# Token factors and first weights made beside the experts, one batch's gating at the attention's end, re-paired PSUM banks

## The chip, the cores and the metric

One core of a Trainium2 chip. The metric is the device time of one execution in microseconds, lower is better. The engines are TensorE (PE, with its weight loads as PEld), VectorE (DVE), ScalarE (ACT), GpSimd (POOL) and SyncE (SP), which here only issues transfers.

## The reference

Linear attention, a mixture of experts with one expert per token, and a feed-forward block, in float32, on 4 batches of 576 tokens with 8 heads of 64:

```python
def phi(x):                       # omega: 128 x 64
    h = x @ omega.T - (x * x).sum(-1, keepdims=True) / 2
    return np.exp(h - h.max(-1, keepdims=True)) / np.sqrt(128)
q_p, k_p = phi(q_s), phi(k_s)
kv, z = k_p^T @ v, k_p.sum(2)     # per batch and head
x = (q_p @ kv) / (q_p @ z + 1e-6) # then 2304 tokens x 512
e = argmax(x @ w_gate)            # 8 experts, softmax weight g
x = g * (relu(x @ w1[e]) @ w2[e]) # 512 -> 1024 -> 512
out = relu(x @ w_in) ** 2 @ w_out # 512 -> 2048 -> 512
```

## The kernel before

Products that need float32 accuracy are made of three fp32r products: each operand is split into a rounded part, which ScalarE copies, and a remainder, which VectorE subtracts (`split`, L688). A split so costs one instruction on each of the two engines, and PE waits for both.

**Attention** (`attention`, L430 on) runs over 18 tiles of 128 tokens; a step `s` works on several tiles at different depths. Since 576 is no multiple of 128, tiles 4 and 13 hold tokens of two batches; `kv_part` (L277) multiplies 64 rows of them for the one batch and 64 for the other. When a batch's logits are complete, `gating` (L387) makes its one-hot choice of experts on DVE, `counting` (L417) sums it with small matmuls and `counted` (L427) gives the batch's commonest expert to POOL as a register. For batches zero and one this is done inside the loop (gating at s = 7 and 11, counting at s = 8 and 12), for two and three beside the first expert steps.

**Experts**: the kernel computes, for each batch, its commonest expert for all of its tokens (another path computes the general case when a token differs, and isn't taken here). The work is 64 steps (batch, half of its tokens, f of 8). `ffn_next` issues layer one of the coming step and its `hidden` part (L765 on ACT, hh; L766 on DVE, hl); `ffn_this` issues layer two of the present step, 24 matmuls in all per step, and then `extras`: what the table that `plan` (L812) made has for this step. Before the first step of another half, `xsplit` (L740, L742) splits four pieces of x. `layer2` (L767) copies y at the last f of a half from PSUM with ACT and stores it to memory (yscr).

**Feed-forward**: blocks of its first product are made with a seven-product scheme: sums of quarter blocks (`lefts`, `rights`, L60 to L72, on POOL), then seven products. 16 stages `first(u)` (L916) of some 11 us have 14 pieces of six matmuls; stages 0 and 1 use the token factors of batches zero and one, stages 2 and 3 those of two and three. A token factor of half (b, c) is loaded from yscr (`x_load`), summed (`x_sums`, POOL) and split (`x_split`); a weight pair likewise (`pair_load`, `pair_sums`, `pair_split`). `raw_place` gives the unsplit data one of two places in turn. The table puts the loads of batches zero and one at steps 48 to 54 and of two and three beside stages 0 and 1. The other DVE work of the expert steps is narrowing of weights (`narrow`, L716 to L720) and the remainder of the expert weights (`wB`, L612).

The second product (`plain`, `second`, L1044) is written in groups of two tiles; the last groups use seven products again, which lie two to a PSUM bank (`PRODS`). `close` (L1065) adds them on DVE, scales by ACT (L1090) and stores by SP (L1091).

The order of each engine's instructions is the order in which this code issues them; the table's step numbers (SA + n is a piece of the feed-forward stages, 14 per stage) fix it.

Of the kernel before, what the change touches and what calls it, by code (L numbers as in the profile page):

```python
# [7 lines left out]
F32 = mybir.dt.float32  # L8
# [7 lines left out]
P = 128  # L16
# [10 lines left out]
KC = DM // P  # L27
VW = D + 1
# [12 lines left out]
PRODS = ((1, 0, 0, 0, 0), (6, 4, 4, 1, 0), (7, 5, 5, 1, 1), (5, 3, 3, 2, 0), (3, 6, 1, 2, 1), (4, 1, 6, 3, 0), (2, 2, 2, 0, 1))  # L41
# [48 lines left out]
class Kern:  # L90
# [36 lines left out]
    def setup_attn(self):  # L127
# [9 lines left out]
        self.hl, self.three = {}, {}  # L137
        w = self.qpool.tile([P, 2 * M], F32, name="wom")
# [29 lines left out]
    def load_v(self, t):  # L168
        if t >= NT:
            return  # L170
        v = self.vin[t] = self.kpool.tile([P, H, VW], F32, tag="vin", name=f"vin{t}", bufs=5)
        self.nc.sync.dma_start(out=v, in_=self.a["vv"][t])
# [104 lines left out]
    def kv_part(self, b, t, i):  # L277

        nc = self.nc
# [3 lines left out]
        lo, hi = [(lo, hi) for bb, lo, hi in pieces(t) if bb == b][0]  # L283
        for j in range(4):
            nc.tensor.matmul(  # L285
                self.kv_ps[b, i][:, j * VW : (j + 1) * VW],
                self.kp[t][lo:hi, 4 * i + j, :],
                self.vin[t][lo:hi, 4 * i + j, :],
# [127 lines left out]
    def counting(self, b):  # L416

        nc = self.nc
        ps = self.banks(f"cnt_ps{b}")[:, 0, :] if b > 1 else self.bank("x", f"cnt_ps{b}")
# [20 lines left out]
    def attention(self, beside):  # L440
# [13 lines left out]

        def gating(last):
            self.gating((0, 5, 9, 14)[(4, 8, 13, 17).index(last)], last + 1)
# [46 lines left out]
        for s in range(13):  # L503
# [13 lines left out]
            if s - 4 in (4, 8):  # L517
                self.counting((4, 8).index(s - 4))
# [15 lines left out]
            if s - 3 in (4, 8):  # L534
                gating(s - 3)
            if s - 4 in (4, 8):
                self.counted((4, 8).index(s - 4))
# [94 lines left out]
    def pair_load(self, layer, p):  # L632

        raw = self.raw[layer, p] = self.raw_place(2 * P)
# [134 lines left out]
    def layer2(self, st):  # L769
# [14 lines left out]
        if last:  # L784
            t0 = b * S + hf * HALF
            y = self.four(f"y{b}_{hf}")
# [33 lines left out]
    def plan(self):  # L820
# [19 lines left out]
        for i in range(4):  # L840
            b, c, u = i // 2, i % 2, 48 + 2 * i
            at(u, self.x_load, b, c)
            at(u + 2, self.x_sums, b, c)
            for j in range(4):
                at(u + 3 + j // 2, self.x_split, b, c, j)
        at(57, self.pair_load, 1, 0)
        at(58, self.pair_sums, 1, 0)
        for i in range(4):
            at(60 + i // 2, self.pair_split, 1, 0, i)

        at(61, self.pair_load, 1, 1)
        at(62, self.pair_sums, 1, 1)
        for i in range(4):
            at(SA + 2 + i, self.pair_split, 1, 1, i)
        beside = ((1, 4, 9, 10, 11, 12), (5, 9, 14, 15, 15, 16), (12, 17, 20, 21, 22, 23), (16, 21, 25, 25, 26, 27))
        for i, (l, m, *f) in enumerate(beside):
            b, c = 2 + i // 2, i % 2
            at(SA + l, self.x_load, b, c)
            at(SA + m, self.x_sums, b, c)
            for j in range(4):  # L860
                at(SA + f[j], self.x_split, b, c, j)
# [24 lines left out]
    def x_load(self, b, c):  # L886

        raw = self.raw["x", b, c] = self.raw_place(HALF)
        src = self.yscr[:, c::2, b * S : (b + 1) * S]
        queue = self.nc.gpsimd if b == 3 else self.nc.sync  # L890
        queue.dma_start(out=raw[:, 0:4].rearrange("p (h j) t -> p h (j t)", h=2), in_=src)
        if c == 0:
            n = 14 * HALF
            big = self.big[b // 2][:, b % 2 * 2 * n : (b % 2 + 1) * 2 * n].bitcast(F32R)
            self.xc[b] = [big[:, i * n : (i + 1) * n].rearrange("p (k c t) -> p k c t", k=7, c=2) for i in range(2)]

# [167 lines left out]
    def close(self, g, m):  # L1064
# [24 lines left out]
        for t, o in ((2 * g, o2), (2 * g + 1, o1)):  # L1089
            nc.scalar.activation(o, o, AF.Copy, scale=self.g2[:, t : t + 1])  # L1090
            nc.sync.dma_start(out=self.o["out"][t * P : (t + 1) * P, :], in_=o)  # L1091
# [58 lines left out]
def main_path(k, tc, a, o):  # L1150
    nc = k.nc
    with ExitStack() as ctx:
# [39 lines left out]
        k.gating(9, 14)  # L1192
# [99 lines left out]
```

## Time and profile before

| | us |
|---|---|
| median of 3 runs (lowest, highest) | 759.24 (758.96, 762.48) |
| profiled execution | 761.62 |
| its span in the profile | 760.1 |
| PE busy | 738.2 (97%) |
| DVE busy | 568.7 (75%) |
| ACT busy | 419.1 (55%) |
| POOL busy | 222.1 (29%) |

The span begins with the first and ends with the last instruction that the profiler recorded; 1.5 us of the execution lie around it. The mean granted clock of PE is 0.988 of full speed. In a timeline row, the bracket at the end is the time that the engine stood before this instruction and what released it.

### The profile page before, as it was taken

Reading aid. Unit: us, or ns where it says so; the run is one execution under the profiler, and the core shown is the slowest. Engines: PE = TensorE matmul, PEld = TensorE weight load, DVE = VectorE, ACT = ScalarE, POOL = GpSimd, SP = SyncE. Lnnn points to the kernel's source line nnn. Section 1 sums busy time; section 2 is a strip of 40 time slices with the busy share of each in tenths; the row PEclk is TensorE's granted clock in tenths of the full one; section 3 lists DMA queues with packets and bytes.
Section 4 is the critical chain, followed back from the end, with each engine's and each line's share of the span. In section 5 each row is a group of like instructions: output and inputs, shape, how many; then the busy total and the mean of one; then the engine's idle time right before and its main releaser. Section 6 shows DMA issues by size and latency. Waiting matters only on the chain. (4 is left out here: it accounts for less than half of the span.)

```text
span 760.1 us, 15737 instructions
## 1 busy us (share of the span) xinstructions
PE 738.2 (97%) x5832; PEld 729.8 (96%) x5832; DVE 568.7 (75%) x1204; ACT 419.1 (55%) x1012; POOL 222.1 (29%) x292
## 2 busy tenths in 40 slices
PE   8999999999999999999997999999999999999995
PEld 7999998999999999999997999999999999999995
DVE  7888877876776677668297768778685799888792
ACT  5878776963555345435464645555573365454451
POOL 4765666831100000037176115232431110000000
PEclk9999998999999999999998999999999999999998
DMA  8756654645866766552244446556868374444430
GB/s 298 240 187 194 189 183 125 184 123 165 266 203 187 260 212 211 199 181 91 89 157 147 167 167 216 194 194 209 284 222 270 118 225 144 136 140 134 127 98 31
DMA packets 76467, 136.14 MB, mean 179 GB/s; under 512 B 8512, under 2 KB 37328, under 8 KB 76384
## 3 DMA queue, kind: packets, MB, share of 16 engines
q1 hardware_dynamic: 64704, 94.48, 37.9%
q0 software_dynamic: 11680, 40.59, 17.1%
q8 instruction: 48, 0.79, 0.4%
q14 instruction: 35, 0.29, 0.1%
HBM read 93.54 MB, written 41.50 MB: 178 GB/s over the span
## 5 line engine op out<-in xcount | busy, mean ns | idle before, releaser
L765 ACT ACTIVATE hh<-h 128x288 fp32r<-128x288 f32 x64 | 26.4, 412 | 98.5 <-PE h L755 98.4
L766 DVE SCALAR_TENSOR_TENSOR hl<-h,hh 128x288 fp32r<-128x288 f32 x64 | 29.1, 455 | 42.5 <-ACT hh L765 42.1
L922 ACT COPY xT<-X 128x288 f32<-128x288 f32 x96 | 37.1, 400 | 38.5 <-PE X L948 38.3
L1016 ACT CAST hc<-xT 128x384 fp32r<-128x384 f32 (+1 forms) x76 | 38.8, 563 | 28.9 <-DVE xT L63 20.4
L272 ACT ACTIVATE kp<-pj_kp,bias_kp 128x128 f32<-128x128 f32 x144 | 39.4, 398 | 25.1 <-DVE bias_kp L260 16.6
L618 POOL DMA_DIRECT2D we<-we x32 | 17.7, 554 | 121.2 <-DVE wB L612 54.3
L1062 PE MATMUL y<-wB,hc 128*128 128x256 f32 x152 | 43.2, 284 | 0.0
L1060 PE MATMUL y<-wB,hc 128*128 128x256 f32 x152 | 43.1, 284 | 0.0
L1061 PE MATMUL y<-wB,hc 128*128 128x256 f32 x152 | 43.0, 283 | 0.0
L1018 DVE TENSOR_TENSOR hc<-xT,hc 128x384 fp32r<-128x384 f32 (+1 forms) x76 | 42.2, 617 | 0.0
L947 PE MATMUL X<-wB,w 128*128 128x288 f32 x128 | 38.4, 300 | 3.4 <-DVE wB L691 3.4
L272 ACT ACTIVATE qp<-pj_qp,bias_qp 128x128 f32<-128x128 f32 x144 | 39.4, 396 | 3.2 <-DVE rd L364 1.5
L285 PE MATMUL kv_ps<-vin,kp 128*128 128x65 f32 (+1 forms) x320 | 40.4, 280 | 0.0
L925 DVE SCALAR_TENSOR_TENSOR xT<-xT 128x288 f32<-128x288 f32 (+1 forms) x64 | 40.2, 661 | 0.0
L946 PE MATMUL X<-wA,w 128*128 128x288 f32 x128 | 38.2, 298 | 1.7 <-ACT xT L922 1.2
L285 PEld LDWEIGHTS kv_ps<-vin,kp 128*128 128x128 f32 (+1 forms) x320 | 38.7, 196 | 1.1 <-issue 0.3
L754 PE MATMUL h<-xl,wB 128*128 128x288 f32 x128 | 38.2, 298 | 1.0 <-DVE xl L742 1.0
L946 PE MATMUL X<-wB,w 128*128 128x288 f32 x128 | 38.4, 300 | 0.4 <-ACT wB L690 0.4
L754 PE MATMUL h<-xl,wA 128*128 128x288 f32 x128 | 38.0, 297 | 0.4 <-DVE xl L742 0.4
L782 PE MATMUL y<-hl,wA 128*128 128x288 f32 x128 | 37.9, 296 | 0.3 <-DVE hl L766 0.3
L753 PE MATMUL h<-xh,wA 128*128 128x288 f32 x128 | 38.2, 298 | 0.0
L948 PE MATMUL X<-wB,w 128*128 128x288 f32 x128 | 38.1, 297 | 0.0
(242 smaller groups left out, 3032.6 us busy)
## 6 DMA issues: line engine op xcount, KB each, us to landing
hscr<-xT SPq DMA_DIRECT2D x32, 576.0 KB, 3.7
we<-we POOLq DMA_DIRECT2D x32, 512.0 KB, 4.8
xT<-hscr SPq DMA_DIRECT2D x64, 256.0 KB, 4.4
xT<-wscr POOLq DMA_DIRECT2D x48, 256.0 KB, 4.1
wd<-wf SPq DMA_DIRECT2D x22, 512.0 KB, 5.1
wscr<-narrow SPq DMA_DIRECT2D x22, 256.0 KB, 2.3
wd<-wf POOLq DMA_DIRECT2D x10, 512.0 KB, 4.4
vin<-vv SPq DMA_DIRECT2D x18, 260.0 KB, 4.1
```

The lines of the kernel that those rows point to most:

```text
L272: nc.scalar.activation(y[:, h, :], ps[h // 4][:, h % 4 * M : (h % 4 + 1) * M], AF.Exp, bias=bias[:, h : h + 1])
L285: nc.tensor.matmul(self.kv_ps[b, i][:, j * VW : (j + 1) * VW], self.kp[t][lo:hi, 4 * i + j, :], self.vin[t][lo:hi, 4 * i + j, :], start=(t ...
L753: nc.tensor.matmul(ps, w1, xh, start=(c == 0), stop=False)
L754: nc.tensor.matmul(ps, w1, xl, start=False, stop=False)
L925: nc.vector.scalar_tensor_tensor(v, v, 0.0, v, op0=ALU.max, op1=ALU.mult)
L946: nc.tensor.matmul(ps, w1, xh[:, r, c], start=(start and c == 0), stop=False, skip_group_check=True)
L947: nc.tensor.matmul(ps, w1, xl[:, r, c], start=False, stop=False, skip_group_check=True)
L1016: nc.scalar.copy(hc[q].at(0, a, b), raw[:, q, a + 1 : b + 1])
L1018: nc.vector.tensor_tensor(hc[q].at(1, a, b), raw[:, q, a + 1 : b + 1], hc[q].at(0, a, b).bitcast(F32), ALU.subtract)
L1060: nc.tensor.matmul(ps, h1, w1, start=first, stop=False, skip_group_check=True)
L1061: nc.tensor.matmul(ps, h1, w2, start=False, stop=False, skip_group_check=True)
L1062: nc.tensor.matmul(ps, h2, w1, start=False, stop=last, skip_group_check=True)
```

## The change

1. `PRODS` puts the seven products into other pairs of banks: product 2, the last to be computed, has one for itself, products 1 and 6, 7 and 5, 4 and 3 share one each. `close` scales in halves of 256 columns, and stores the very last tile in two parts.
2. `kv_part` uses all 128 rows: the v of the two straddling tiles is loaded into two places whose other 64 rows were set to zero at the start.
3. Batch one's gating is made together with batch two's behind the loop, its counting beside the first expert steps; batch two's counting comes one step later.
4. The x loads go through POOL's queue, into four places given by a table. Batches zero to two are loaded, summed and split at expert steps 34 to 61, the first weight pairs at 49 to the first pieces. Batch three's y is copied from PSUM into its place directly; only its sums and splits are beside stage 0.

```diff
-PRODS = ((1, 0, 0, 0, 0), (6, 4, 4, 1, 0), (7, 5, 5, 1, 1), (5, 3, 3, 2, 0), (3, 6, 1, 2, 1), (4, 1, 6, 3, 0), (2, 2, 2, 0, 1))
+PRODS = ((1, 0, 0, 0, 0), (6, 4, 4, 0, 1), (7, 5, 5, 1, 0), (5, 3, 3, 1, 1), (4, 1, 6, 2, 0), (3, 6, 1, 2, 1), (2, 2, 2, 3, 0))
...
+        self.halves = [self.xT_flat[:, at : at + H * VW].rearrange("p (h w) -> p h w", h=H) for at in (3 * KC * S, 3 * KC * S + H * VW)]
+        nc.gpsimd.memset(self.halves[0][64:P], 0.0)
+        nc.gpsimd.memset(self.halves[1][0:64], 0.0)
...
+        if len(pieces(t)) == 2:
+            self.vin[t] = self.halves
+            for i in range(2):
+                rows = slice(i * 64, (i + 1) * 64)
+                self.nc.sync.dma_start(out=self.halves[i][rows], in_=self.a["vv"][t, rows])
+            return
...
-                self.kp[t][lo:hi, 4 * i + j, :],
-                self.vin[t][lo:hi, 4 * i + j, :],
+                self.kp[t][:, 4 * i + j, :],
+                self.vin[t][part][:, 4 * i + j, :],
...
-            if s - 4 in (4, 8):
-                self.counting((4, 8).index(s - 4))
+            if s - 4 == 4:
+                self.counting(0)
...
-            if s - 3 in (4, 8):
-                gating(s - 3)
-            if s - 4 in (4, 8):
-                self.counted((4, 8).index(s - 4))
+            if s - 3 == 4:
+                self.gating(0, 5)
+            if s - 4 == 4:
+                self.counted(0)
...
+        if p < 2:
+            at = (2 + p) * RAW
...
+            if b == B - 1:
+                if hf == 0:
+                    self.last = [self.x_place(b, c) for c in range(2)]
+                for d in range(KC):
+                    nc.scalar.copy(self.last[d % 2][:, d // 2 * 2 + hf], acc[d][:, :HALF])
+                return
...
-        for i in range(4):
-            b, c, u = i // 2, i % 2, 48 + 2 * i
-            at(u, self.x_load, b, c)
-            at(u + 2, self.x_sums, b, c)
+        for b, c, l, m, f in ((0, 0, 34, 38, 43), (0, 1, 36, 40, 45), (1, 0, 45, 47, 48), (1, 1, 47, 49, 51), (2, 0, 56, 57, 59), (2, 1, 55, 58, 60)):
+            at(l, self.x_load, b, c)
+            at(m, self.x_sums, b, c)
             for j in range(4):
-                at(u + 3 + j // 2, self.x_split, b, c, j)
-        at(57, self.pair_load, 1, 0)
-        at(58, self.pair_sums, 1, 0)
...
-        beside = ((1, 4, 9, 10, 11, 12), (5, 9, 14, 15, 15, 16), (12, 17, 20, 21, 22, 23), (16, 21, 25, 25, 26, 27))
...
+                at(f + j // 2, self.x_split, b, c, j)
+        for p, l, m, f in ((0, 49, 51, 53), (1, 61, 62, SA)):
+            at(l, self.pair_load, 1, p)
+            at(m, self.pair_sums, 1, p)
             for j in range(4):
-                at(SA + f[j], self.x_split, b, c, j)
+                at(f + (j if p else j // 2), self.pair_split, 1, p, j)
+
+        for c, m, f in ((0, SA, SA + 5), (1, SA + 4, SA + 10)):
+            at(m, self.x_sums, 3, c)
+            for j in range(4):
+                at(f + j, self.x_split, 3, c, j)
...
-        queue = self.nc.gpsimd if b == 3 else self.nc.sync
...
+        region = (((0, 1), (0, 1), (3, 2), (0, 1))[b][c]) * RAW
...
+        self.nc.gpsimd.dma_start(out=self.x_place(b, c)[:, 0:4].rearrange("p (h j) t -> p h (j t)", h=2), in_=src)
...
-            nc.scalar.activation(o, o, AF.Copy, scale=self.g2[:, t : t + 1])
-            nc.sync.dma_start(out=self.o["out"][t * P : (t + 1) * P, :], in_=o)
+            for c in (slice(0, n), slice(n, 2 * n)):
+                nc.scalar.activation(o[:, c], o[:, c], AF.Copy, scale=self.g2[:, t : t + 1])
+                if g == NG - 1 and o is o1 or c.start:
+                    w = c if g == NG - 1 and o is o1 else slice(0, 2 * n)
+                    nc.sync.dma_start(out=self.o["out"][t * P : (t + 1) * P, w], in_=o[:, w])
...
         k.x_step(NT - 1)
-        k.gating(9, 14)
+        k.gating(5, 14)
         k.ffn_next()
+        k.ffn_this()
+        k.counting(1)
+        k.counted(1)
+        k.ffn_next()
+        k.gating(14, 18)
         k.ffn_this()
         k.counting(2)
         k.counted(2)
```

How the instructions of VectorE stand at three places (the names are those of the tiles written and read). The first is attention step 11, before:

```order
L260 TENSOR_REDUCE bias_kp_1936<-three_kp_1881 128x8
L393 TENSOR_REDUCE gmx_1947<-lg 128x4
L395 TENSOR_TENSOR gsh_1949<-lg,gmx_1947 128x32
L399 SCALAR_TENSOR_TENSOR gfi_1952<-gsh_1949,rank 128x32
L401 TENSOR_REDUCE gfm_1954<-gfi_1952 128x4
L402 TENSOR_TENSOR oneh<-gfi_1952,gfm_1954 128x32
L364 TENSOR_SCALAR rd_1959<-n_ps_1960 128x8
L365 RECIPROCAL rd_1959<-rd_1959 128x8
```

and changed:

```order
L270 TENSOR_REDUCE bias_kp_1938<-three_kp_1883 128x8
L375 TENSOR_SCALAR rd_1951<-n_ps_1952 128x8
L376 RECIPROCAL rd_1951<-rd_1951 128x8
L377 TENSOR_TENSOR xr_1949<-n_ps_1952,rd_1951 128x512
L378 TENSOR_TENSOR lgh_1950<-n_ps_1952,rd_1951 128x64
```

The five operations from `gmx` to `oneh`, batch one's choice, have gone from between the bias of the keys and the logits (`rd` to `lg`) of the next tile.

The second is the turn from batch two's last to batch three's first expert step; `xl` is the remainder of x, `wB` that of an expert weight, `hl` that of the hidden layer, for which layer two waits. Before:

```order
L742 TENSOR_TENSOR xl_0_3_4546<-xT,xh_0_3_4545 128x288
L717 TENSOR_SCALAR narrow_4563<-narrow_4563 128x512
L718 TENSOR_SCALAR narrow_4563<-narrow_4563 128x512
L719 SCALAR_TENSOR_TENSOR narrow_4563<-wd_4474,narrow_4563 128x512
L720 SCALAR_TENSOR_TENSOR narrow_4563<-wd_4474,narrow_4563 128x512
L612 TENSOR_TENSOR wB<-we_6_4476,wB 128x1024
L766 SCALAR_TENSOR_TENSOR hl_0_0_4586<-h_0_0_4572,hh_0_0_4585 128x288
L766 SCALAR_TENSOR_TENSOR hl_0_1_4623<-h_0_1_4609,hh_0_1_4622 128x288
```

and changed (L704 is what L691 was, the remainder of a token factor, L779 what L766 was, L755 what L742 was):

```order
L755 TENSOR_TENSOR xl_0_3_4561<-xT,xh_0_3_4560 128x288
L730 TENSOR_SCALAR narrow_4578<-narrow_4578 128x512
L731 TENSOR_SCALAR narrow_4578<-narrow_4578 128x512
L732 SCALAR_TENSOR_TENSOR narrow_4578<-wd_4480,narrow_4578 128x512
L733 SCALAR_TENSOR_TENSOR narrow_4578<-wd_4480,narrow_4578 128x512
L620 TENSOR_TENSOR wB<-we_6_4482,wB 128x1024
L704 TENSOR_TENSOR wA<-xT,wA 128x2x288
L704 TENSOR_TENSOR wA<-xT,wA 128x288
L779 SCALAR_TENSOR_TENSOR hl_0_0_4605<-h_0_0_4591,hh_0_0_4604 128x288
L779 SCALAR_TENSOR_TENSOR hl_0_1_4647<-h_0_1_4633,hh_0_1_4646 128x288
```

Between the weight's remainder and `hl_0_0` two operations of a token factor have come in; two more (not shown) stand before the `xl` rows.

The third is the second feed-forward stage (u = 1), where Z and Y are its PSUM tiles. Before:

```order
L956 TENSOR_TENSOR xT<-Z_0_5332,xT 128x288
L691 TENSOR_TENSOR wB<-xT,wB 128x2x288
L956 TENSOR_TENSOR xT<-Z_1_5333,xT 128x288
L691 TENSOR_TENSOR wB<-xT,wB 128x2x288
L959 TENSOR_TENSOR xT<-xT 128x288
L691 TENSOR_TENSOR wB<-xT,wB 128x2x288
L959 TENSOR_TENSOR xT<-xT 128x288
L691 TENSOR_TENSOR wB<-xT,wB 128x288
```

and changed:

```order
L971 TENSOR_TENSOR xT<-Z_0_5351,xT 128x288
L971 TENSOR_TENSOR xT<-Z_1_5352,xT 128x288
L974 TENSOR_TENSOR xT<-xT 128x288 x2
L976 TENSOR_TENSOR xT<-Y_0_5353,xT 128x288
L940 SCALAR_TENSOR_TENSOR xT<-xT 128x288
L976 TENSOR_TENSOR xT<-Y_1_5354,xT 128x288
L940 SCALAR_TENSOR_TENSOR xT<-xT 128x288
```

The remainders of token factors (L691) that stood between the stage's own additions are gone from it.

## Rows read from the trace of the kernel before

**Rows 1.** The page: busy time and instructions of each engine; granted clock in 40 slices

```profile
...
PE 738.2 (97%) x5832; PEld 729.8 (96%) x5832; DVE 568.7 (75%) x1204; ACT 419.1 (55%) x1012; POOL 222.1 (29%) x292
...
PEclk9999998999999999999998999999999999999998
...
```

**Rows 2.** Timeline, 116 to 124 us: start, duration, instruction, idle before it

```profile
...
119.33 0.99 DVE L402 TENSOR_TENSOR oneh<-gfi,gfm 128x32 f32<-128x32 f32 x1
...
121.64 1.06 PE L336 MATMUL t_ps<-ident,qp 128*128 128x128 f32 x8 [1.55 <-DVE lgh L367]
...
```

**Rows 3.** Windows: busy time (x instructions) of each engine, clock, DMA

```profile
...
122.00:132.00 10.00, 10.00 (x69) 9.79 (x68) 6.17 (x21) 4.56 (x18) 4.78 (x6) 0.66 0.41 126
...
```

**Rows 4.** Timeline of PE, 80 to 86 us

```profile
...
84.26 1.06 PE L336 MATMUL t_ps<-ident,qp 128*128 128x128 f32 x8 [0.85 <-DVE lgh L367]
...
```

**Rows 5.** Windows, 396 to 412 us

```profile
...
396.00:404.76 8.76, 3.78 (x23) 3.04 (x23) 8.70 (x14) 5.82 (x13) 6.79 (x9) 0.92 0.30 97
404.76:412.00 7.24, 7.24 (x36) 7.24 (x37) 3.24 (x6) 2.47 (x7) 4.26 (x7) 0.63 0.66 237
...
```

**Rows 6.** Timeline, 396 to 412 us

```profile
...
400.32 0.86 POOL L69 TENSOR_TENSOR xT<-xT 128x288 f32<-128x288 f32 x1 [1.81 <-DMA xT<-yscr]
...
404.76 0.61 PE L947 MATMUL X<-wB,w 128*128 128x288 f32 x1 [3.37 <-DVE wB L691]
...
```

**Rows 7.** Timeline of DVE, 311 to 350 us, expert steps

```profile
...
315.84 0.46 DVE L766 SCALAR_TENSOR_TENSOR hl<-h,hh 128x288 fp32r<-128x288 f32 x1 [0.27 <-ACT hh L765]
316.77 1.23 DVE L612 TENSOR_TENSOR wB<-we,wB 128x1024 fp32r<-128x1024 f32 x1 [0.48 <-ACT wB L609]
319.04 0.46 DVE L766 SCALAR_TENSOR_TENSOR hl<-h,hh 128x288 fp32r<-128x288 f32 x1 [1.04 <-ACT hh L765]
319.42 1.55 DVE L742 TENSOR_TENSOR xl<-xT,xh 128x288 fp32r<-128x288 f32 x4
...
321.87 0.69 DVE L719 SCALAR_TENSOR_TENSOR narrow<-wd,narrow 128x512 int32<-128x512 int32 x1
...
324.34 0.45 DVE L766 SCALAR_TENSOR_TENSOR hl<-h,hh 128x288 fp32r<-128x288 f32 x1
...
331.80 1.28 DVE L719 SCALAR_TENSOR_TENSOR narrow<-wd,narrow 128x512 int32<-128x512 int32 x1
...
335.58 1.54 DVE L691 TENSOR_TENSOR wA<-xT,wA 128x576 fp32r<-128x576 f32 x2
...
345.28 3.10 DVE L742 TENSOR_TENSOR xl<-xT,xh 128x288 fp32r<-128x288 f32 x4
348.30 1.11 DVE L691 TENSOR_TENSOR wA<-xT,wA 128x576 fp32r<-128x576 f32 x2
...
```

**Rows 8.** Waits of PE: total, times, longest, in us

```profile
...
PE h L754 <- DVE xl L742: 1.4, 4, 0.4
...
```

**Rows 9.** Timelines of PE, 56 to 66 and 98 to 110 us

```profile
...
59.90 1.90 PE L285 MATMUL kv_ps<-vin,kp 128*128 128x65 f32 x16
...
101.78 4.21 PE L285 MATMUL kv_ps<-vin,kp 64*128 64x65 f32 x32
...
```

**Rows 10.** Groups of POOL's instructions, 331 to 361 us

```profile
...
L69 POOL TENSOR_TENSOR xT<-xT 128x288 f32<-128x288 f32 x4 | 4.5, 1123 | 19.7 <-DMA xT<-yscr 19.7
...
```

**Rows 11.** Timeline, 750.9 us to the end

```profile
...
751.95 0.28 PE L1062 MATMUL y<-wA,hc 128*128 128x256 f32 x1
...
754.88 1.38 ACT L1090 ACTIVATE o<-o,g 128x512 f32<-128x512 f32 x2 [2.19 <-DVE o L1080]
755.05 0.41 DVE L1080 TENSOR_TENSOR o<-y,p 128x256 f32<-128x256 f32 x1
...
```

**Rows 12.** Timeline of PE, 318 to 328 us

```profile
...
324.91 0.33 PE L782 MATMUL y<-hl,wB 128*128 128x288 f32 x1
...
```

**Rows 13.** DMA issues: KB each, median us from issue to landing

```profile
...
xT<-yscr POOLq DMA_DIRECT2D x2, 576.0 KB, 5.3
...
```

**Rows 14.** The page: costliest groups of instructions

```profile
...
L618 POOL DMA_DIRECT2D we<-we x32 | 17.7, 554 | 121.2 <-DVE wB L612 54.3
...
```

More of the change, by code (lines that the diff above doesn't have):

```diff
@@ L170, in load_v @@
             return
-        v = self.vin[t] = self.kpool.tile([P, H, VW], F32, tag="vin", name=f"vin{t}", bufs=5)
+        if len(pieces(t)) == 2:
[4 more added lines that the diff above has]
+            return
+        v = self.kpool.tile([P, H, VW], F32, tag="vin", name=f"vin{t}", bufs=5)
+        self.vin[t] = [v]
         self.nc.sync.dma_start(out=v, in_=self.a["vv"][t])
@@ L282, in kv_part @@
             self.kv_ps[b, i] = self.bank(f"w{i}", f"kv_ps{b}_{i}")
-        lo, hi = [(lo, hi) for bb, lo, hi in pieces(t) if bb == b][0]
+        part = [bb for bb, lo, hi in pieces(t)].index(b)
         for j in range(4):
@@ L418, in counting @@
         nc = self.nc
-        ps = self.banks(f"cnt_ps{b}")[:, 0, :] if b > 1 else self.bank("x", f"cnt_ps{b}")
+        ps = self.banks(f"cnt_ps{b}")[:, 0, :] if b > 0 else self.bank("x", f"cnt_ps{b}")
         parts = [(t, lo, hi) for t in range(NT) for bb, lo, hi in pieces(t) if bb == b]
@@ L453, in kv @@
                 self.kv_close(ends[s])
-        def gating(last):
-            self.gating((0, 5, 9, 14)[(4, 8, 13, 17).index(last)], last + 1)
         self.warm()
@@ L632, in pair_load @@
     def pair_load(self, layer, p):
-        raw = self.raw[layer, p] = self.raw_place(2 * P)
+        if p < 2:
+            at = (2 + p) * RAW
+            raw = self.xT_flat[:, at : at + 16 * P].rearrange("p (k c) -> p k c", k=8)
+        else:
+            raw = self.raw_place(2 * P)
+        self.raw[layer, p] = raw
         for i in range(2):
@@ L884, in place, with x_place @@
         return Factor(v[:2], v[2:])
-    def x_load(self, b, c):
-        raw = self.raw["x", b, c] = self.raw_place(HALF)
-        src = self.yscr[:, c::2, b * S : (b + 1) * S]
-        queue = self.nc.gpsimd if b == 3 else self.nc.sync
-        queue.dma_start(out=raw[:, 0:4].rearrange("p (h j) t -> p h (j t)", h=2), in_=src)
+    def x_place(self, b, c):
+        region = (((0, 1), (0, 1), (3, 2), (0, 1))[b][c]) * RAW
+        raw = self.raw["x", b, c] = self.xT_flat[:, region : region + RAW].rearrange("p (k t) -> p k t", k=8)
         if c == 0:
@@ L895, in x_load @@
             self.xc[b] = [big[:, i * n : (i + 1) * n].rearrange("p (k c t) -> p k c t", k=7, c=2) for i in range(2)]
+        return raw
+    def x_load(self, b, c):
+        src = self.yscr[:, c::2, b * S : (b + 1) * S]
+        self.nc.gpsimd.dma_start(out=self.x_place(b, c)[:, 0:4].rearrange("p (h j) t -> p h (j t)", h=2), in_=src)
     def x_sums(self, b, c):
@@ L1196, in main_path @@
         k.counted(2)
-        k.ffn_next()
-        k.gating(14, 18)
-        k.ffn_this()
         k.ffn_next()
```

10 lines of the change are left out of this document (removed).

## The prediction

> **What bounds the kernel now.** I first read the page's busy times and slices. TensorE is busy for 738.2 of 760.1 us [rows 1], so almost nothing is gained by making other engines cheaper; what counts is the 22 us in which TensorE stands, and the time in which it runs at half clock. The line of the granted clock has only three slices below nine tenths: the 7th (114 to 133 us), the 22nd (399 to 418) and the last [rows 1]. So I read, in that order, the timeline at the end, the timeline around 120 us, and that around 400 us, each for the instruction that TensorE waited for; then the waits of TensorE as a list, and VectorE's timeline in the expert steps that the change loads with more work.
>
> All sums are made on the profiled execution, 761.62 us, which lies 2.4 us above the median of 759.24. A half-clock spell of some 7 to 10 us more or less, as priced below, is about that difference. A measurement of this kernel can tell some 0.5% from no change: below 755.44 is faster, above 763.04 slower.
>
> **The change, part by part.**
>
> *Batch one's gating leaves the attention loop.* In the loop VectorE computes batch one's one-hot choice just before the gate logits of the next tile; its last product ends at 120.32, and TensorE stands 1.55 us for the logits, until 121.64 [rows 2]. From 122 to 132 TensorE is busy all the time, but at a granted clock of 0.66, a mix of its two levels, 2.4 and 1.2 GHz [rows 3]: 10.00 x 0.34 = 3.4 us. Batch zero's gating, which stays, also makes TensorE stand, for 0.85 us [rows 4], and there the clock's slice is not low [rows 1]. Without the five VectorE operations the wait goes, and with it the spell: **-4.97** (ends: -1.55, if the spell comes anyway, and -4.97). At the attention's end the same operations are done for nine tiles at once instead of five, and one more counting; that is beside the first expert steps, and nothing asks for batch one's choice before step 3's weight load. I take 0; if that cover were gone, the price is about that of the loop, 1.55.
>
> *Tokens' factors before the first weights' stages.* In these stages, 16 of some 11 us, every product needs the token factors of two batches, split in two parts by ScalarE and VectorE; the third stage is the first to need batches two and three. Now these are made beside the second stage: from 396 to 404.76 TensorE is busy for 3.78 of 8.76 us, so it stands 4.98, and in the next 7.24 us the clock is 0.63, which costs 7.24 x 0.37 = 2.68 [rows 5]. The longest wait, 3.37 us, is for VectorE's split of a factor, which itself came late because POOL's sums waited 1.81 for the transfer of batch three's y from memory [rows 6]. After the change batches zero to two are loaded and split beside the expert steps, and batch three's y is copied from PSUM straight into its place, with no trip through memory. Stage two then has only batch three's second half to split. **-7.66** (ends: -4.98 and -7.66; the rival is below).
>
> *Fewer sums beside the split of x.* At the last change of x halves VectorE's four xl operations took 3.10 us beside POOL's token sums, against 1.55 where POOL was not adding [rows 7], and TensorE waited for xl 1.4 us in four waits [rows 8]. After the change POOL's sums lie earlier. **-1.0** (ends: 0 and -1.4).
>
> *v with zero rows.* The two tiles that straddle two batches are now multiplied with all 128 rows, their other half zero. 16 passes of 128 rows take 1.90 us, 32 of 64 rows 4.21 [rows 9]: no more for a full pass than for half a one. Each of the two tiles has 32 passes: 2 x (4.21 - 2 x 1.90) = **-0.8** (ends: 0, if the full passes lose what the half ones did, and -0.8). The Trainium skill, page "TensorE: Matmul & The Clock Gate", section "Part 3: Packing small matmuls — row/col tiling", says that matmuls with few rows placed in different row groups run at once; by that, filling up the rows would lose an overlap, and the sum would be about 4 x 0.95 = 3.8 us (an estimate: half the passes' time, four times) the other way instead. The trace does not agree: 32 passes of 64 rows in 4.21 us show no overlap. The two added memsets on POOL and two more v loads on SP come tiles ahead of their use: 0; uncovered, the memsets are no dearer than two POOL additions, 2.2 us [rows 10].
>
> *Banks re-paired, stores halved.* At the end the last matmul starts at 751.95; ScalarE scales two tiles of 512 columns in 1.38 us from 754.88, VectorE's last addition of seven is at 755.05, and the span closes at 760.1 [rows 11]. With product 2 alone in its bank, all additions but one can be done earlier. What is left behind the last matmul: about 0.4 to get to VectorE, one addition of 0.41 and half a scaling of 0.69, then the store of a half. ScalarE would then end at some 753.2 where it ended at 756.26: 3.06. I take **-3.0** (ends: -2.0, if two or three more additions of 0.41 stay behind; -3.6, if the smaller last store lands sooner). Halves of scaling in the other groups are ScalarE's, which is busy 55%: 0.
>
> *What the expert steps have to carry.* This is the part that costs. One expert step is some 3.2 us, and VectorE's remainder (hl) must be ready when layer two starts. For step 48, the first of batch three, hl is computed from 324.34 to 324.79 [rows 7], and TensorE's matmul that reads it starts at 324.91 [rows 12]: 0.1 us, no slack. Into the 9 us before, the change puts the second half of the split of batch zero's first factor (1.11 us), and both halves of the second (1.54 and 1.11): 3.76 us, by the rows of two wide pieces and of a wide and a narrow one [rows 7]. VectorE was idle there for 0.27 + 0.48 + 1.04 = 1.79 [rows 7]. So hl comes 1.97 late. Beside it POOL now adds batch one's sums (four operations of about 1.04 us, by the four means of [rows 10], of which the first is shown), and VectorE operations with two inputs from SBUF suffer from that: the narrowing's went from 0.69 to 1.28 us [rows 7]. 4.2 us at that ratio lose 4.2 x (1 - 0.69/1.28) = 1.9, together 3.9. I take **+3.5** (ends: +2.0 and +4.1), nearer to the upper end, since the loads for these sums are issued one step ahead and the sums last a whole step. The Trainium skill, page "GPSIMD Engine Reference", section "8. Key points", says that GpSimd shares its SBUF interfaces with VectorE and that they contend when VectorE has two SBUF inputs; the row with 1.28 agrees. By this rule the term is the 3.9, without it 2.0.
>
> *Other steps.* Two narrowings (steps about 38 and 40) get POOL's sums beside them: 2 x 0.59 each, less the idle of such a step, 0.27 + 0.48: 2 x 0.43 = **+0.9** (ends 0 and 2.4). SP loses six loads and two writes of y; POOL's queue gets four x loads more, each 5.3 us from issue to landing [rows 13], among its weight loads.
>
> Sum: 761.62 - 4.97 - 7.66 - 1.0 - 0.8 - 3.0 + 3.5 + 0.9 = **748.6 us**.
>
> **The rivals.**
>
> *A half-clock spell comes anew.* Where TensorE stood 1.55 us or more in one place, half clock followed twice [rows 2, 3, 5]; where it stood 0.85, not. If the stall at step 48 comes in one piece of 3.5 us, it may do the same: +3.4, 752.0. Against it: the joint near 400 stood in several pieces, and the wait may be spread over steps 46 to 48. Chance 0.34.
>
> *VectorE keeps up.* The splits of two parts may start earlier than I place them, ahead of a ScalarE copy for which VectorE now waits anyway. Then neither stall comes: 748.6 - 3.5 - 0.9 = 744.2. For it: VectorE stands idle 1.0 to 1.8 in every unloaded step. Chance 0.14.
>
> *The joint stays.* If batch three's factors are still late (POOL's sums wait for the last y copies, then eight splits run beside two stages), the 7.66 are not gained: 756.3, within 0.5%. Against it: the copies are done ahead of the first stage, two stages of 11 us before the need. Chance 0.07.
>
> *Slower: the POOL queue.* x loads now stand behind the weight loads on POOL's queue, which wait, over 32 of them, 121.2 us for a free stage, 54.3 of it for VectorE's weight split [rows 14]. A load that stands behind one of these holds back the sums (4.2 us), and ScalarE's copy and VectorE's split wait with hl queued behind them. Between load and second split of batch one's first half lie four steps, 12.8 us, against 5.3 + 4.2 = 9.5; a delay over 3.3 us decides. Each miss costs a chain of 4.2 and a spell of 3.4, 7.6; two are needed to be slower by more than 0.5% (763.8), four give 779.0. Chance 0.03.
>
> **How the numbers follow.** Forecast 0.42, new spell 0.34, no stall 0.14, joint stays 0.07, POOL queue 0.03. Faster by more than 0.5%: 0.42 + 0.34 + 0.14 = 0.90; same 0.07; slower 0.03. The range goes from 743.0 (no stall, with the tail at its better end and the joint complete) to 753.0 (the new spell, with the stall at its upper end), and leaves out the last two cases and the far ends.
>
> **What would show it right or wrong.** Right: no wait of VectorE's lgh over 1 us near 120, with a granted clock near 1 from 122 to 132; no wait of TensorE for a factor's split near 400; the last scaling under 1.5 us behind the last matmul; a new wait of TensorE for hl near step 48, of 2 to 4 us. Wrong: a slice of low clock near 320; xT loads on POOL that land after their sums are due; ScalarE waiting for POOL's xT ahead of hh; or 128-row passes dearer than 1.90 per 16.

## The result and the profile after

The changed kernel took 753.35 us (median of 5 runs, 751.44 to 758.81); the kernel before, timed beside it, 762.48 (758.96 to 765.87). The ratio is 0.9902, with a 95% interval of 0.9873 to 0.9932: faster by 1.0%, where 748.6 us (0.983 of the profiled 761.62) had been forecast, and 0.35 us above the stated range. Sign and mechanism of the large terms were right, about a third of the gain was lost on the way.

The profiled execution of the changed kernel is its slowest, 758.81 us (span 757.3). So a second one was profiled later (first experiment below, 752.54 us), and the two are read side by side. The page, engines and granted clock in 40 slices; the lines answer to [rows 1]:

```profile
PE 735.0 (97%) x5832; PEld 727.3 (96%) x5832; DVE 566.2 (75%) x1199; ACT 421.6 (56%) x1025; POOL 223.3 (29%) x298
...
PEclk9999999999999999999999999999999989999999
...
```

The low slices at 114 and 399 us are gone; a new one stands at 606 to 625. TensorE's waits (total, times, longest):

```profile
PE h L767 <- DVE xl L755: 4.4, 7, 1.4
PE y L1075 <- ACT o L1090: 3.6, 1, 3.6
PE y L795 <- DVE hl L779: 3.5, 4, 1.8
```

The 3.4 us for the factor's split near 400 [rows 6] is no longer in the list, nor the 1.55 us for the logits [rows 2]. In their place stand waits for xl and hl in the expert steps, and one for a scaling (o) at the start of the second product.

Where the time came from and went is read by following one instruction through both traces: the start of ScalarE's hidden-layer copy of a step, of its square in a stage, and of TensorE's matmuls behind that, in us.

| place | before | changed | difference | second profile, difference |
|---|---|---|---|---|
| hidden layer, step 0 | 161.32 | 156.04 | -5.28 | -4.48 |
| step 10 | 200.35 | 196.19 | -4.15 | -2.57 |
| step 41 | 299.42 | 299.39 | -0.04 | -0.32 |
| step 56 | 349.03 | 353.26 | +4.23 | +2.84 |
| third stage's square | 416.94 | 412.78 | -4.16 | -5.56 |
| second product, first matmul | 562.70 | 558.53 | -4.17 | -5.56 |
| second product, four groups on | 634.23 | 634.33 | +0.09 | -6.44 |
| end of the span | 760.07 | 757.27 | -2.80 | -9.16 |

From one row to the next the change's parts come out by themselves: attention -5.28, the joint of the stages -8.4 and the tail -2.9 are gains; the first ten steps (+1.1), steps 10 to 41 (+4.1), 41 to 56 (+4.3) and the start of the second product (+4.3) are losses. In the second profile the last is a gain of 0.9, and the execution, 9.2 us faster, is near the median.

### The profile page after: what moved, and what is told of

Same layout as the page of the kernel before. It is cut to its first block, busy times and chain, and to the rows that moved or that the text cites. A ratio compares the mean times of both kernels' runs of the same rounds, so it can differ in the third digit from the quotient of the medians.

```text
span 757.3 us, 15759 instructions
## 1 busy us (share of the span) xinstructions
PE 735.0 (97%) x5832; PEld 727.3 (96%) x5832; DVE 566.2 (75%) x1199; ACT 421.6 (56%) x1025; POOL 223.3 (29%) x298
## 4 chain that ended last, share of the span: by engine, by line
PE 74%; DVE 10%; DMA 7%; issue 4%; ACT 4%; SPq 0%; POOL 0%; DVEq 0%; ACTq 0%; POOLq 0%
PE y L1075 6%; PE y L1077 6%; PE y L1076 6%; PE X L961 4%; PE X L963 4%; PE X L962 4%; PE kv_ps L296 3%; PE h L767 3%; PE h L768 3%; PE n_ps L367 3%; PE h L766 3%; PE y L795 3%; PE y L796 3%; PE y L794 3%; PE Z L961 2%
## 5 line engine op out<-in xcount | busy, mean ns | idle before, releaser
L779 DVE SCALAR_TENSOR_TENSOR hl<-h,hh 128x288 fp32r<-128x288 f32 x64 | 28.9, 454 | 42.6 <-ACT hh L778 42.4
L1075 PE MATMUL y<-wB,hc 128*128 128x256 f32 x152 | 43.7, 288 | 0.0
L1076 PE MATMUL y<-wB,hc 128*128 128x256 f32 x152 | 43.7, 287 | 0.0
L1077 PE MATMUL y<-wB,hc 128*128 128x256 f32 x152 | 43.7, 287 | 0.0
L795 PE MATMUL y<-hl,wB 128*128 128x288 f32 x128 | 37.9, 296 | 1.0 <-DVE hl L779 1.0
L794 PE MATMUL y<-hh,wA 128*128 128x288 f32 x128 | 38.5, 301 | 0.0
L940 DVE SCALAR_TENSOR_TENSOR xT<-xT 128x288 f32<-128x288 f32 (+1 forms) x64 | 38.2, 634 | 0.0
L796 PE MATMUL y<-hh,wA 128*128 128x288 f32 x128 | 38.2, 298 | 0.0
L766 PE MATMUL h<-xh,wA 128*128 128x288 f32 x128 | 38.2, 298 | 0.0
L766 PE MATMUL h<-xh,wB 128*128 128x288 f32 x128 | 37.9, 296 | 0.0
L961 PE MATMUL X<-wB,w 128*128 128x288 f32 x128 | 37.9, 296 | 0.0
```

The costliest lines, as they stand in the source:

```text
L766: nc.tensor.matmul(ps, w1, xh, start=(c == 0), stop=False)
L794: nc.tensor.matmul(out, w1, hh, start=(f == 0), stop=False)
L795: nc.tensor.matmul(out, w1, hl, start=False, stop=False)
L796: nc.tensor.matmul(out, w2, hh, start=False, stop=last)
L961: nc.tensor.matmul(ps, w1, xh[:, r, c], start=(start and c == 0), stop=False, skip_group_check=True)
L1075: nc.tensor.matmul(ps, h1, w1, start=first, stop=False, skip_group_check=True)
```

## The losses as the trace shows them

**xl beside the sums.** VectorE's four xl operations for step 40, and POOL's sums of batch zero's first factor, in the timeline of the changed kernel:

```profile
291.14 0.82 POOL L69 TENSOR_TENSOR xT<-xT 128x288 f32<-128x288 f32 x1
...
291.68 3.82 DVE L755 TENSOR_TENSOR xl<-xT,xh 128x288 fp32r<-128x288 f32 x4
...
299.77 0.82 POOL L69 TENSOR_TENSOR xT<-xT 128x288 f32<-128x288 f32 x1
...
300.39 2.01 DVE L730 TENSOR_SCALAR narrow<-narrow 128x512 f32<-128x512 f32 x1
```

Solo, xl took 1.55 [rows 7]. The sums, moved off one half's change of x, fell on two others. The last row is a surprise: this narrowing has one SBUF input and took 0.43 us elsewhere in the same trace, and 2.01 here. The Trainium skill, page "GPSIMD Engine Reference", section "8. Key points", names two cases: VectorE instructions with two SBUF inputs, or in a 2-port mode, contend with GpSimd. The row of xl, with two inputs, agrees; whether the narrowing ran in a 2-port mode, no row shows.

**What TensorE waited for in the expert steps**, from its timeline, in the same trace:

```profile
284.32 0.40 PE L795 MATMUL y<-hl,wA 128*128 128x288 f32 x1 [1.82 <-DVE hl L779]
...
293.84 0.40 PE L767 MATMUL h<-xl,wA 128*128 128x288 f32 x1 [1.30 <-DVE xl L755]
...
322.38 0.40 PE L767 MATMUL h<-xl,wB 128*128 128x288 f32 x1 [1.41 <-DVE xl L755]
...
340.33 0.40 PE L795 MATMUL y<-hl,wB 128*128 128x288 f32 x1 [1.01 <-DVE hl L779]
```

The first has another cause: the narrowing ahead of that hl started at 280.41, after 3.49 us of waiting for ScalarE and so for its weight, whose load is a row of the chain of waits:

```profile
271.80 7.89 DMA wd<-wf
```

Such a load lands in 5.4 us in the median; the x load of 576 KB, which the change put at 267.69, and a y store were in flight. In the second profile the same x load and y store are in flight, the weight's load takes 6.06 us, and the wait isn't there: that the x load alone made it is not shown here (e2 and e8 below come back to it). Behind the stall at step 48 the granted clock fell for some 4 us, which the windows show as 0.57:

```profile
324.00:328.00 4.00, 4.00 (x21) 4.00 (x20) 3.90 (x7) 1.77 (x5) 0.81 (x1) 0.57 0.65 213
```

**The start of the second product**, timeline and window:

```profile
606.55 1.14 ACT L703 CAST wB<-xT 128x512 fp32r<-128x512 f32 x2 [2.00 <-DVE xT L71]
...
607.60 1.26 ACT L1090 ACTIVATE o<-y,g 128x512 f32<-128x512 f32 x2
...
608.33 0.58 PE L1075 MATMUL y<-wA,hc 128*128 128x256 f32 x1 [3.57 <-ACT o L1090]
```

```profile
608.30:614.00 5.70, 5.67 (x26) 5.67 (x27) 5.41 (x14) 3.36 (x7) 0.67 (x2) 0.50 0.81 248
```

TensorE needs the bank of the first group; ScalarE's scaling empties it, but stands in ScalarE's queue behind a split that waits for VectorE's sums. From 600.6 us on VectorE stands for no transfer before this; it is late from the 30 us before, in which its sums waited for theirs. VectorE's waits between 558 and 602 us, in this trace:

```profile
DVE xT L69 <- DMA xT<-wscr: 6.9, 2, 5.0
DVE xT L70 <- DMA xT<-wscr: 5.3, 5, 1.7
```

Before, TensorE's wait was there already, but short:

```profile
PE y L1060 <- ACT o L1075: 0.8, 1, 0.8
```

Over all traces that scale in this order, the wait goes with VectorE's waits for these transfers in the 44 us from the product's first matmul: 3.1 to 3.6 us where they come to 11.3 to 12.3 (the changed kernel, e6, e8, e11), 0.3 to 0.8 where they come to 8.7 to 9.7 (before, e2, e4, e5, e7), none over 0.15 where they are 4.3 (e12). How early TensorE comes does not order them: in e7 it comes 9.6 us before the kernel before and waits 0.43.

## The experiments

The theory: the two stalls with their clock were worth what was forecast, and the rest is lost to three things: POOL's sums beside VectorE's xl and narrowing, x loads ahead of narrowed weights' loads, and the queue of ScalarE at the second product. The rivals are named in each expectation. All edits are to the changed kernel.

**e5, the changed kernel again**, no edit.

> The changed kernel once more, unaltered, beside the next three on one chip. If the spread of its executions (751.4 to 758.8) comes from transfers that land earlier or later, this trace shows other waits than the first one: the 3.57 us at the start of the second product between 0.4 and 3.6, the wait for hl at step 36 there or not, the waits for xl at the same two places. Time 751 to 758.

753.7 us (752.54 to 755.42), ratio 0.9892 (0.9872 to 0.9912). As expected other waits: 0.3 us for the scaling, none for hl at step 36, xl as before:

```profile
PE h L767 <- DVE xl L755: 4.8, 8, 1.3
PE y L795 <- DVE hl L779: 2.3, 3, 1.5
...
PE y L1075 <- ACT o L1090: 0.3, 1, 0.3
```

So the losses in the expert steps are in both traces (5.4 us from step 10 to 56 here, 8.4 in the first), the loss at the second product only in one.

**e4, batch one's gating and counting back in the loop**, the diff cut.

```diff
-            if s - 3 == 4:
-                self.gating(0, 5)
+            if s - 3 in (4, 8):
+                self.gating(*((0, 5), (5, 9))[(4, 8).index(s - 3)])
...
-        k.gating(5, 14)
+        k.gating(9, 14)
...
-        k.counting(1)
-        k.counted(1)
```

> The changed kernel with batch one's gating and counting put back into the attention loop. Theory A (this part is worth the wait of 1.55 us and the half-clock spell behind it, less 1.1 us that the later gating costs beside the first expert steps): the wait for lgh near 121 us is back at about 1.5 us, granted clock about 0.66 from 122 to 132 us, 3 to 5 us slower than the changed kernel in the trace up to step 10. Rival B (the spell comes by chance, it has nothing to do with this wait): only 1.5 us slower there, clock near 1.

The trace has the wait and the half clock back, as in [rows 2, 3]:

```profile
121.38 1.06 PE L347 MATMUL t_ps<-ident,qp 128*128 128x128 f32 x8 [1.54 <-DVE lgh L378]
```

```profile
122.00:132.00 10.00, 10.00 (x69) 9.80 (x67) 6.17 (x21) 4.72 (x17) 4.55 (x6) 0.66 0.37 119
```

At step 0 it stands at -0.27 against before, where the changed kernel has -5.28 and -4.48. But the times, 755.75, 752.00, 756.91 and 753.35 (mean clock 0.993, 0.997, 0.995, 0.998), have a median of 754.55, only one us over the changed kernel's. A fall as in the trace, 10 us at 0.66, takes 3.4 of 754 us and so 0.0045 off an execution's mean clock, so by their clock the fall didn't come in the second and the fourth. So theory A holds where it falls and rival B where it doesn't: the wait of 1.55 us stands in both traces that have this gating in the loop (the other executions left none), the 3.4 are not sure.

The other traces show the same of another wait. At step 48, e1, e5, e9 and e12 have the same three waits for xl, 0.81, 0.3 and 0.3 us. In e1, e9 and e12 the clock is at half for 3.4 us behind them, in e5 it doesn't fall. The first of the waits and the clock, in e5:

```profile
321.52 0.40 PE L767 MATMUL h<-xl,wB 128*128 128x288 f32 x1 [0.81 <-DVE xl L755]
...
324.00:328.00 4.00, 3.74 (x29) 3.50 (x27) 3.90 (x7) 2.35 (x7) 0.49 (x1) 1.00 0.80 240
```

and in e12:

```profile
321.32 0.40 PE L767 MATMUL h<-xl,wB 128*128 128x288 f32 x1 [0.81 <-DVE xl L755]
...
323.80:327.20 3.40, 3.40 (x17) 3.40 (x16) 3.30 (x6) 1.61 (x4) 0.00 (x0) 0.50 0.75 226
```

From step 0 to 10 this kernel loses 0.5 us, where the changed one loses 1.1 and 1.9.

**e6 and e7, sums or splits of batches zero and one left out** (so the stages work on data that isn't theirs).

```diff
-            at(m, self.x_sums, b, c)
+            if b == 2:
+                at(m, self.x_sums, b, c)
```

> The changed kernel without POOL's sums of batch zero's and batch one's token factors (four times four additions left out; the splits read what lies in the place). Theory A (POOL's additions beside VectorE's xl and narrowing are most of what the expert steps lose): xl waits fall from 4.4 to about 1.5 us, hl waits at steps 48 to 50 go; 4 to 5 us less than the changed kernel up to step 56. Rival B (the splits' own time): under 1.5 us less.

```diff
-            for j in range(4):
+            for j in range(4 if b == 2 else 0):
                 at(f + j // 2, self.x_split, b, c, j)
```

> The changed kernel without the splits of batch zero's and batch one's token factors (sixteen ScalarE copies and sixteen VectorE subtractions left out; the feed-forward stages read what lies in the place), the sums kept. Theory A (POOL's additions beside VectorE's xl and narrowing): the xl waits at steps 40 and 48 stay at 1.3 us each, and no more than 2 us are gained. Rival B (the splits' own time): 3.5 us or more are gained, the waits at steps 48 to 50 go.

748.03 us without sums (745.88 to 753.02), 748.12 without splits (747.61 to 751.43); the changed kernel on the same chip 753.7. From step 10 to step 56 the traces lose 0.0 us without the sums, 2.3 without the splits, and 5.4 with both. Without splits, xl at step 40 is as slow as in the changed kernel, and the wait for it stays:

```profile
290.21 3.81 DVE L755 TENSOR_TENSOR xl<-xT,xh 128x288 fp32r<-128x288 f32 x4
...
292.37 0.40 PE L767 MATMUL h<-xl,wA 128*128 128x288 f32 x1 [1.30 <-DVE xl L755]
```

Without sums xl is fast and the wait goes, and one wait for hl stays:

```profile
292.08 1.56 DVE L755 TENSOR_TENSOR xl<-xT,xh 128x288 fp32r<-128x288 f32 x4
...
324.86 0.40 PE L795 MATMUL y<-hl,wB 128*128 128x288 f32 x1 [1.37 <-DVE hl L779]
```

By the traces the sums beside other work are the larger part, as theory A has it: 5.4 us go with them. But neither theory holds alone. The splits give 3.1 in the trace and 5.6 in the time, where A had at most 2 and B 3.5 or more, and the two together would give more than is lost, so that they share some of it.

**e2 and e8, the sums and loads put elsewhere.** Table of loads, sums and splits (b, c, load, sums, split), and batch one's first factor in another place (region 2):

```diff
-(0, 0, 34, 38, 43), (0, 1, 36, 40, 45), (1, 0, 45, 47, 48), (1, 1, 47, 49, 51)
+(0, 0, 26, 33, 43), (0, 1, 33, 41, 45), (1, 0, 41, 43, 48), (1, 1, 47, 49, 51)
```

> The changed kernel, with batch zero's and batch one's first token factors loaded earlier (steps 26, 33, 41) and summed at steps 33, 41, 43, away from the splits of x at steps 38 and 46 and from the narrowed weights' loads behind a y store; pair 0 one step later. Theory A (the expert steps lose 8 us by where POOL's sums and the x load lie, not by the splits themselves): the waits for xl fall from 4.4 to about 2 us, those for hl from 3.5 to about 1, the short half-clock stretch near 324 us goes; about 5 to 7 us less between steps 34 and 56, 746 to 749. Rival B (VectorE's 3.8 us of splits ahead of step 48 are what delays, as the prediction had it): the waits move from xl to hl but keep 3 us or more, gain under 3 us.

749.87 us (748.03 to 751.43), ratio 0.9831 (0.9806 to 0.9856): faster than both kernels, its interval lies below those of the changed kernel. The waits for xl fell to 1.7 us, but those for hl rose to 4.7:

```profile
255.93 0.41 PE L795 MATMUL y<-hl,wB 128*128 128x288 f32 x1 [1.40 <-DVE hl L779]
...
328.18 0.40 PE L795 MATMUL y<-hl,wB 128*128 128x288 f32 x1 [1.46 <-DVE hl L779]
```

The time is 0.9 us above theory A's range, with rival B's trace in part. The first of these waits is at the step behind the new load at 26, and there the weight's load issued 1.5 us behind the x load took 8.01 us (8.33 in e3, which has the same table); in the other twelve traces, without an x load there, it took 5.5 to 6.5. The second table has the loads in gaps between narrowed weights' loads:

```diff
+(0, 0, 16, 20, 43), (0, 1, 30, 33, 45), (1, 0, 41, 43, 48), (1, 1, 47, 50, 52)
```

> The changed kernel with the token factors' loads put into gaps of the narrowed weights' loads (steps 16, 30, 41, 47), their sums at steps without narrowing or a split of x (20, 33, 43, 50), the first pair two steps later. Theory (an x load issued right behind a narrowed weight's load makes that one late, and hl with it): the waits for hl at steps 27 (1.4) and 37 (0.8) of the earlier moved table go, that at step 49 (1.46) falls below 0.8; 746 to 749, one to three us less than that table's 749.9. Rival (the loads are late wherever they are put): 749 to 751.

The wait at step 27 is gone and that at 37 too; the one at step 49 stayed at 1.46, where less than 0.8 was expected. It is there without sums too (e6, 1.37) and not without splits (e7). From step 10 to 56 the loss is 1.9 us, after 4.4 with the first table. Yet the time is 751.5 (749.31 to 752.24), above theory and rival: in the profiled execution TensorE waits 3.2 us at the second product's start. So the theory is right on the two waits behind moved loads, and not on the time.

**e1 and e9, the scaling issued earlier**: right behind the plain product, or between the coming split and the sums.

```diff
+            if pp == 3 and n < PLAIN:
+                k.close(g, k.ys.pop(g))
             k.h_load(n + 3)
...
-            if pp == 3:
+            if pp == 3 and n >= PLAIN:
                 k.close(g, k.ys.pop(g))
```

> The changed kernel, with the scaling and storing of the first two groups (close) issued right behind their last plain product instead of behind the next split and sums. Theory A (the 3.57 us for which TensorE waits at 608 us come from ScalarE's queue: the scaling that frees the PSUM bank stands behind copies that wait for VectorE's sums, and these for transfers): the wait falls below 0.8 us, the half-clock stretch behind it (0.50 over 5.7 us, about 3 us) goes with it; about 3 to 6 us less than the changed kernel where that execution had the spell, 2 to 3 less where it had not, so 748 to 751. Rival B (the split hidden parts of the next group come too late whatever ScalarE does): the wait only changes its name to hc, time as the changed kernel's, 751 to 755.

> The changed kernel with the first two groups' scaling issued between the split of the coming hidden part and the next sums. Theory A (a scaling ahead of the hidden part's split delays that split, as the wait of 1.2 us for hc in the first form showed; one ahead of the sums alone delays nothing that TensorE wants): wait for the scaling under 0.8 us in the profile, none for hc, and no execution above 754; median 751.5 to 753. Rival B: the waits are set by the transfers of the sums, and come back as a wait for hc of 1 us or more; median 752.5 to 754.

Medians 753.15 (752.78 to 754.79) and 755.11 (752.03 to 756.98): no gain. The wait for the scaling is gone, and one for the hidden part hc has come, the first row of e1's trace, the second of e9's:

```profile
620.24 0.39 PE L1077 MATMUL y<-wA,hc 128*128 128x256 f32 x1 [1.23 <-DVE hc L1033]
```

```profile
623.74 0.39 PE L1077 MATMUL y<-wA,hc 128*128 128x256 f32 x1 [1.82 <-DVE hc L1033]
```

Rival B's wait is there in both; e9's median lies above both of its forecasts. In these two traces the order in ScalarE's queue decides only under which name TensorE waits. That the sums' transfers set the pace is read from the waits above; no run changed them.

**e3 and e10, combinations**: e1's order with e2's table, e9's with e8's.

> Both edits together. If the waits are independent, the gains add up: 743 to 747, with a granted clock of 0.998 or more. Rival: what is gained in the expert steps is waited for again at the start of the second product, because its sums are paced by their transfers: gain of the table's edit alone, 748 to 750.

> The table in the gaps together with the scaling issued between. If the first removes some 4 us of the expert steps and the second the 3.2 us at the start of the second product, 746.5 to 749.5, the fastest of all that compute everything; if the latter wait comes back as one for hc, 749 to 751.

750.76 us (750.32 to 751.43; ratio 0.9849, 0.9826 to 0.9871) and 750.16 us (749.78 to 752.37; 0.9846, 0.9801 to 0.9892). Both as the rivals have it (e3 0.8 us above its rival's range): no more than the table alone gives. e10 stands 10.2 us before the kernel before at the second product's first matmul and 9.1 four groups on, with 1.8 us of waiting for hc. e2, e3, e8 and e10 cannot be told apart.

**e11, the old bank pairs and whole scalings.** `PRODS` and the end of `close` as before the change.

> The changed kernel with the products' old bank pairs and whole scalings and stores. Theory (the end gains 3 us because only one addition and half a scaling are left behind the last matmul): the last scaling ends about 4.3 us behind the start of the last matmul instead of 1.4, and the time is 2.5 to 3.3 us longer than the changed kernel's 753.5: 756 to 757. Rival (the rest of the engines' queues hides it): under 1 us longer.

757.18 us (754.85 to 759.53, 10 runs), 3.5 over e5's median. The tail of the changed kernel and that of e11, timelines:

```profile
751.50 1.91 ACT L1106 ACTIVATE o<-o,g 128x256 f32<-128x256 f32 x4 [2.31 <-DVE o L1095]
...
752.05 0.28 PE L1077 MATMUL y<-wA,hc 128*128 128x256 f32 x1
...
752.36 0.42 DVE L1095 TENSOR_TENSOR o<-y,p 128x256 f32<-128x256 f32 x1
```

```profile
749.73 0.28 PE L1077 MATMUL y<-wA,hc 128*128 128x256 f32 x1
...
752.66 1.39 ACT L1105 ACTIVATE o<-o,g 128x512 f32<-128x512 f32 x2 [2.19 <-DVE o L1095]
```

The scaling ends 1.4 us behind the start of the last matmul, where it ended 4.3 behind: theory, 2.9 us by the traces. The times alone don't settle it, since the ratios' intervals overlap (0.9901 to 0.9944 here, 0.9872 to 0.9912 in e5). What the new pairs give and what the halved scalings and stores was not tried apart.

**e12, batch three's y through memory**, the rest as changed; sums 9 pieces later.

```diff
-            if b == B - 1:
-                if hf == 0:
-                    self.last = [self.x_place(b, c) for c in range(2)]
...
-        for c, m, f in ((0, SA, SA + 5), (1, SA + 4, SA + 10)):
+        for c, m, f in ((0, SA + 9, SA + 14), (1, SA + 13, SA + 19)):
+            at(SA + 1 + c, self.x_load, 3, c)
```

> The changed kernel with batch three's y stored to memory and loaded back, as before the change, everything else as changed; sums and splits nine pieces later. Theory A (the joint's gain of 8.4 us comes from batches zero to two being done beside the experts, which leaves two stages, 22 us, for batch three): no wait over 1 us at the third stage, time as the changed kernel's, 752 to 755, or up to 0.5 us less at the first stage, where TensorE waits for the copies. Rival B (the direct copy is what saves it): the wait for the split near 400 us is back with 2 us or more, and a half-clock stretch behind it; 756 to 760.

752.95 us (751.2 to 754.91), as the changed kernel, and TensorE is busy throughout the joint:

```profile
390.00:402.00 12.00, 12.00 (x92) 12.00 (x91) 12.00 (x18) 8.71 (x21) 7.94 (x8) 1.00 0.35 124
402.00:408.00 6.00, 6.00 (x47) 6.00 (x46) 3.35 (x6) 3.66 (x10) 5.47 (x7) 1.00 0.59 222
```

Theory A: the joint's stall is gone without the direct copy, which gives nothing. What ended it is the work done beside the experts, batches zero to two and with them the first weight pairs; these two were not tried apart.

## Why the prediction was right in parts and wrong in the sum

| step of the prediction | forecast | first profile | second |
|---|---|---|---|
| gating and v with zero rows (to step 0) | -5.8 | -5.3 | -4.5 |
| gating at the end, "I take 0" (steps 0 to 10) | 0 | +1.1 | +1.9 |
| other steps (10 to 41) | +0.9 | +4.1 | +2.3 |
| step 48's stall, less the xl gain (41 to 56) | +2.5 | +4.3 | +3.2 |
| joint | -7.7 | -8.4 | -8.4 |
| start of the second product | none | +4.3 | -0.9 |
| tail | -3.0 | -2.9 | -2.7 |
| sum | -13.0 | -2.8 | -9.2 |

- **Joint and tail** were right in size. Of the joint's two reasons, e12 leaves the work done earlier; the copy without a trip through memory was worth nothing. The 0.7 us more in the joint fit what the 4.98 us left out, since they count only TensorE's standing: in the 8.76 us of [rows 5] its 23 matmuls were busy for 3.78 us, and at the pace of the stretch behind (47 in 6.00) they take 2.9.

```profile
412.00:418.00 6.00, 6.00 (x47) 6.00 (x46) 4.60 (x10) 2.24 (x6) 2.78 (x5) 1.00 0.54 177
```

  The tail's sum had a slip: 751.95 and the three parts named give 753.45, not 753.2, so 2.8 and not 3.06; measured were 2.9 and 2.7.
- **Gating** was right in the trace, and over-sized as a mean. The spell of 3.4 us was counted for sure; e4 shows that it doesn't come in each execution. And its new place was not free: steps 0 to 10 lose 1.1 to 1.9 us, with waits for xl and hl of 0.2 to 0.9 each, and 0.5 with batch one's gating and counting back in the loop (e4). What of the rest is the nine-tile gating and what the moved counting was not tried apart.
- **v with zero rows** was priced from a misread row. The 4.21 us of [rows 9] are a merged row that shows the shape of its first matmul; of its 32 matmuls 16 have 64 rows and 16, of the next tile, have 128, in turn by groups of eight. The groups by shape in that stretch, and the next instruction, before:

```profile
L285 PE MATMUL kv_ps<-vin,kp 128*128 128x65 f32 x16 | 2.2, 281 | 0.0
L285 PE MATMUL kv_ps<-vin,kp 64*128 64x65 f32 x16 | 2.2, 278 | 0.0
...
105.79 0.36 PE L243 MATMUL pj_kp<-womh,kph 128*128 128x256 f32 x1
```

  and the same stretch changed:

```profile
101.48 1.00 PE L296 MATMUL kv_ps<-xT,kp 128*128 128x65 f32 x8
...
104.11 1.06 PE L296 MATMUL kv_ps<-vin,kp 128*128 128x65 f32 x8
104.97 0.36 PE L253 MATMUL pj_kp<-womh,kph 128*128 128x256 f32 x1
```

  One matmul takes the same with 64 rows as with 128; the 32 in changing shapes took 4.01 us to the next instruction, in one shape 3.49. A group of 16 of 64 rows alone, one step earlier, took 1.93, and of 128 rows 1.71. So a tile saves 0.7 us where these stand; some 0.1 at the first tile and 0.5 at the second are left a step on. e4, which has the zero rows without the moved gating, stands at -0.27 at step 0, where -0.8 had been forecast. Nor do these rows speak against an overlap of different row groups: a batch's matmuls in such a tile all use the same 64 rows.

- **The step that failed** is what the expert steps have to carry, with "Other steps". The stall came, at the step foreseen, 3.8 us with its short fall of the clock against 3.5; but it waits first for xl, not for hl (1.7 us in the first profile, 1.4 in the second), and the wait for hl comes a step later and in the second profile only, 1.5. It was taken that the sums move away from the splits of x and give 1.0 us back. By the table they go from one change of half (step 56, where 1.4 us were gained) to two others (40 and 48); at step 40 alone this costs 2.1 us in both profiles, where "Other steps" had 0.9 for narrowings. And an x load's bandwidth was costed at nothing, though narrowed weights come in all along: behind one, such a weight's load took 8 us in e2 and e3, and TensorE waited 1.4 and 1.7 for hl. Forecast +3.4 from step 10 to 56; measured +8.4 and +5.4, 6 to 7 in the other traces with this table.
- **The rivals**: "A half-clock spell comes anew" came in the first profile, twice, near 324 and 608 us; "VectorE keeps up" did not; the joint didn't stay; no wait of TensorE in the two lists goes back to POOL's queue. The wait at the second product's start was no rival at all, though its row, shown above, stood in the list of waits before, with 0.8 us. It was a small sample of a wait that the sums' transfers move between none and 3.6 us.
- **The range** ended 0.35 us too low, since its upper end took the spell and the stall's far end, but none of the small costs that had been put at nothing.

## What to carry to other kernels

Where work is moved into stages that seem to have slack, lay each engine's moved instructions against the steps they will run beside, operation by operation: what counts is not the slack of a mean step but whether a GpSimd addition falls beside a VectorE operation that TensorE is about to want. A small wait in the profile before, behind an engine that is fed by transfers, can come out several times as long in another execution of the same kernel: give it a range in the sum, also where the change doesn't touch it. And a row that merges instructions shows the shape of the first; ask for the groups by shape before taking a price from it. A fall of the clock that follows a wait in one trace should be counted as a chance, not as a cost.

## What was not expected of the hardware

A narrowing with a single SBUF input went from 0.43 to 2.01 us beside POOL's additions. Matmuls of 64 rows in turn with matmuls of 128 took longer than as many of 128 rows, 4.01 against 3.49 us for 32, though one by one they take the same. The same three waits at step 48 were followed by 3.4 us at half clock in three traces and by none in a fourth; and a wait of 1.55 us was followed by 10 us at a clock of 0.66 in two profiled executions, while two other executions of e4 kept a mean clock of 0.997 and 0.998 (whether the wait was there in those, no trace shows).
